# One attention-then-FFT-convolution kernel: pair 3 turned in f32, no key or query rounded by GpSimd, the last two output tiles in halves, all steps in a new order

## The chip, the cores and the metric

The kernel runs on one core of one Trainium2 chip. The metric is the device time of one execution in microseconds, median over the runs. The engines of the core work side by side, each through its own queue in order: TensorE (PE in the profile, its weight loads PEld), VectorE (DVE), ScalarE (ACT), GpSimd (POOL) and SyncE (SP), which here only issues DMAs.

## What is computed

The reference has two parts. Each of the 4 batches has 8 heads of 768 rows and 64 columns. The first part is attention over chosen blocks: the mean key of each block of 64 rows gives a gate score per query, the three best blocks and the query's own block are kept, and the causal softmax runs over those alone.

```python
k_rep = k.reshape(B, H, 12, 64, D).mean(axis=3)
gate_scores = einsum('bhsd,bhnd->bhsn', q, k_rep)      # causal blocks only
sel = top 3 blocks of a query, and its own block
scores = where(mask & causal, q @ k.T / 8, -1e9)
x = softmax(scores) @ v                                # (4, 768, 512)
proj = x @ w_proj                                      # x1, x2, x3, 512 columns each
x2_conv = irfft(rfft(x2, axis=1) * rfft(filter_fft, axis=0), n=768, axis=1)
out = (x1 * x2_conv * x3) @ w_out                      # float32
```

## The kernel before

**Work and tiles.** Heads go in pairs: 16 pairs, four to a batch; pair p holds heads 2*dc and 2*dc+1 of batch b, p = 4*b + dc. A pair's keys and queries come as one f32 tile each (`l`, two DMAs, one per head; line 565), its values by GpSimd's queue as f16 (`lv`, line 558). The scores of a pair are made in three groups (`s3p` to `s3p+2`, lines 802 to 816): keys against queries, then a second product that adds the mask. Each group fills two wide PSUM tiles (tags A and B, one per head); ScalarE takes the exponential of each (`e`, line 822), GpSimd zeroes what lies above the diagonal (`a`, line 828), TensorE multiplies by the values (`p`, line 838), VectorE divides (`nr`, `nm`). `xt`, or `xp` and `xq`, turns the result; `f` folds it (line 890). Then a batch goes through projection (`x`, `x1_`, `x3_`), a real transform written as matrix products (`z`, `t`, `mc`, `m`, `w`), its inverse (`i`, `ic`, `iy`, `iz`), the gate (`gg`, `y`), and the output product (`o`, lines 1034 to 1041), its eviction (`oc`) and store (`od`). Steps `fr`, `ff`, `fz`, `h`, `su`, `sv` transform the filter once.

**Two ways to prepare a pair.** For the pairs in `TURNED` (line 158: 0, 1 and 2) the f32 tiles are turned on TensorE as they are: `kt` multiplies the keys by an identity with two columns more, which give the block sums (line 599), `kh` and `kq` evict, `qt` and `qc` do the same for the queries (lines 589 and 652), `tq` casts a copy to f16, and the gate product `g` takes f32 operands (line 760). For all other pairs the rows are rounded to f16 first: `kn` and `qn` (lines 664, 666, 720, 722) round, `kl` and `qr` (lines 672, 728) keep what the rounding lost, `kw`/`kv` and `qw`/`qv` turn on TensorE and evict (in some pairs one DMA, `kx` or `qx`, does it), `kp`/`kq` sum the blocks, and `g` is 15 f16 products (line 765).

**What sets the order.** Nothing is planned at build time: `ORDER`, a list of 1,432 names, is walked at the end (lines 1081 to 1087). `name:V`, `:A` or `:G` says which engine does the step, `/a` to `/d` which PSUM tile it writes, `zeros/d:40` issues 40 products of zeros. Each engine gets its steps in that order and waits inside them; so a step that waits holds all that stand behind it on its engine. SP issues the loads and stores in list order too. Ten tiles hold loaded keys and queries, eight hold exponentials.

Of the kernel before, what the change touches and what calls it, by code (L numbers as in the profile page):

```python
# [45 lines left out]
kn9:A qr8:V s17 xc0.2:A nr9:V kq8:V nm9:V kr8:G xc0.1:A mt6/d qw7.1/c xt4 e17.0:A x0.3/b z0.0.2:V
lw2.3:G z0.0.1:V e17.1:A kl9:V x0.4/a lk10 qv7.1:A a17.0:G xc0.3:V s15 a16.1:G xc0.4:A z0.0.3:V g7/b
z0.0.0:V mm6:A qx8 z0.1.0:G e15.0:A t0.0.0/a mx7:V x0.5/d e15.1:A a15.0:G t0.1.0/c z0.1.2:V
x1_0.0.0/b xc0.5:A a17.1:G mc0.0.0:V a15.1:G mc0.1.0:A s19 z0.1.3:V lq10 x1c0.0.0:A a16.0:G m0.1.0:V
qn9:A lv6:G p15.1/c m0.0.0:V t0.0.1/b kw8/a m0.0.3:V mc0.0.1:A p15.0/d z0.1.1:V p16.1 kv8:A p17.1  # L50
m0.0.1:V p16.0 nr11:V x1_0.1.1/b m0.1.3:V e19.0:A w0.0.0:G nm11:V p17.0 kp9/a x1c0.1.1:V e19.1:A
# [1070 lines left out]
```

## Time and profile before

| | |
|---|---|
| median of 3 runs | 227.08 us (226.75 to 228.03) |
| the profiled execution | 228.22 us, span from first to last instruction 226.5 us |
| busy: PE, DVE, ACT, POOL | 213.2, 203.0, 175.8, 135.9 us |
| mean granted clock of TensorE | 0.97 of full speed |
| q, k: DMA issues | 64 of 192 KB, 5.3 to 5.4 us to landing (median) |

Busy time is read beside the span; a busy PE is not one at its peak, since ends of matmuls are modelled. The granted clock is 1.00 at 2.4 GHz and 0.50 at 1.2 GHz. "s4" and the like are the steps named above; the trace shows lines, and the first product of such a step is a line 808 instruction.

### The profile page before, as it was taken

What the parts mean: (1) busy time and instruction counts of PE and PEld (TensorE: products, weight loads), DVE (VectorE), ACT (ScalarE), POOL (GpSimd) and SP (SyncE); (2) the same over time, 40 slices, a digit from 0 to 9 for tenths busy, and PEclk for the clock granted to TensorE, in tenths of its full rate; (3) what the DMA queues carried; (4) which work ended last, traced back from release to release, by engine and by line L of the source; (5) the groups of instructions that cost most, each with busy time, mean ns of one, the idle gap of its engine ahead of it and who ended that gap; (6) DMA issues with size and microseconds to landing.
All of it is one profiled execution on the core that took longest, in us unless ns stands there. A gap on an engine that the chain in (4) does not pass through costs nothing.

```text
span 226.5 us, 7238 instructions
## 1 busy us (share of the span) xinstructions
PE 213.2 (94%) x2799; PEld 138.1 (61%) x2799; DVE 203.0 (90%) x656; ACT 175.8 (78%) x281; POOL 135.9 (60%) x260
## 2 busy tenths in 40 slices
...
GB/s 167 265 243 218 213 189 205 168 197 110 97 83 73 147 126 98 184 81 139 212 156 138 205 148 152 126 195 83 135 40 163 96 36 93 142 46 1 157 128 228
DMA packets 104194, 32.19 MB, mean 142 GB/s; under 512 B 97248, under 2 KB 100320, under 8 KB 104160
## 3 DMA queue, kind: packets, MB, share of 16 engines
...
q0 software_dynamic: 27392, 5.25, 30.1%
...
## 4 chain that ended last, share of the span: by engine, by line
PE 67%; DVE 22%; DMA 4%; issue 2%; ACT 2%; SPq 1%; DVEq 0%; ACTq 0%
PE x2p L906 9%; PE op L1039 9%; PE x1p L1006 8%; PE x3p L1018 7%; PE sps L808 7%; PE o L838 6%; PE sps L814 4%; DVE kl L672 2%; DMA nat<-in_k_dram 2%; DVE xnat L861 2%; DMA nat<-in_q_dram 2%; DVE m L774 2%; PE yeo L967 2%; DVE sd L982 1%; PE mt L789 1%
## 5 line engine op out<-in xcount | busy, mean ns | idle before, releaser
L822 ACT ACTIVATE ex<-sps 128x896 f16<-128x896 f32 x96 | 85.1, 923 | 15.2 <-PE sps L814 14.1
L828 POOL TENSOR_SCALAR_AFFINE_SELECT ex<-ex 128x256 f16<-128x256 f16 x96 | 45.8, 489 | 33.5 <-ACT ex L822 31.4
L838 PE MATMUL o<-V,ex 128*128 128x65 f16 x672 | 29.3, 194 | 0.5 <-POOL ex L828 0.4
L838 PEld LDWEIGHTS <-ex 128*128 128x128 f16 x672 | 25.6, 98 | 5.4 <-POOL ex L828 0.5
L808 PE MATMUL sps<-TQ,KH 64*128 64x256 f16 (+2 forms) x352 | 27.9, 272 | 0.2
L558 POOL DMA_DIRECT2D V<-in_v_dram x32 | 27.5, 860 | 0.2
L808 PEld LDWEIGHTS <-KH 64*128 64x128 f16 x352 | 13.2, 95 | 13.8 <-issue 9.7
L1025 DVE TENSOR_TENSOR gg<-x1sb,x3p 128x384 f16<-128x384 f16 x32 | 17.3, 545 | 1.9 <-PE x3p L1018 1.6
L192 ACT COPY osb<-op 128x512 f32<-128x512 f32 x21 | 12.4, 592 | 7.8 <-PE op L1039 5.6
L814 PE MATMUL sps<-MT,E 32*128 32x256 f16 (+2 forms) x480 | 17.5, 229 | 0.0
L861 DVE TENSOR_TENSOR xnat<-o,rc 128x384 f16<-128x384 f32 x32 | 17.2, 547 | 0.2
L192 ACT CAST x1sb<-x1p 128x384 f16<-128x384 f32 x27 | 13.0, 493 | 5.0 <-PE x1p L1006 4.9
L1006 PEld LDWEIGHTS <-wp 128*128 128x128 f16 x128 | 11.5, 97 | 8.0 <-issue 0.8
L1018 PEld LDWEIGHTS <-wp 128*128 128x128 f16 x128 | 11.9, 98 | 6.9 <-DVE lt L776 0.2
L814 PEld LDWEIGHTS <-E 32*128 32x128 f16 x480 | 10.5, 93 | 9.1 <-issue 8.8
L192 ACT CAST yes<-yeo 128x384 f16<-128x384 f32 x23 | 10.6, 483 | 6.1 <-PE yeo L967 5.7
L774 DVE MAX8 m<-g 128x8 f32<-128x12 f32 x160 | 13.8, 156 | 1.2 <-PE g L765 0.7
L672 DVE SCALAR_TENSOR_TENSOR kl<-nat,kn 128x768 f16<-128x768 f32 x13 | 13.8, 1060 | 0.3 <-ACT kn L664 0.2
L991 POOL TENSOR_TENSOR mid<-sd 128x256 f16<-128x256 f16 x5 | 3.7, 735 | 16.3 <-DVE sd L982 16.3
L782 POOL TENSOR_TENSOR MN<-lt,ownm 128x120 f16<-128x120 f16 x12 | 5.8, 481 | 12.2 <-DVE lt L776 11.6
L728 DVE SCALAR_TENSOR_TENSOR qn<-nat,qn 128x640 f16<-128x640 f32 x13 | 10.9, 847 | 0.5 <-POOL qn L722 0.4
L695 PE MATMUL qw<-id,qn 128*128 128x128 f16 x55 | 5.3, 238 | 2.7 <-DVE qn L722 1.6
...
## 6 DMA issues: line engine op xcount, KB each, us to landing
nat<-in_q_dram SPq DMA_DIRECT2D x32, 192.0 KB, 5.3
nat<-in_k_dram SPq DMA_DIRECT2D x32, 192.0 KB, 5.4
...
```

Source lines behind the costliest of these rows:

```text
L192: {"A": nc.scalar.copy, "V": nc.vector.tensor_copy, "G": nc.gpsimd.tensor_copy, "S": nc.sync.dma_start}[eng](dst, src)
L558: nc.gpsimd.dma_start(v16[:, :, h, 0:D], v[b, 2 * dc + h].rearrange("(c p) d -> p c d", p=P))
L808: nc.tensor.matmul(t[x][:, col:col + w], lhsT=kh[rows, P * kc:P * (kc + 1)], rhs=every_other(tq, rows, q0, w), start=(col, kc) == part[0][:2],
L814: nc.tensor.matmul(t[x % 2][:, col:col + w], lhsT=E4[rows, P * kc:P * (kc + 1)], rhs=mt16.rearrange("p c s -> p (c s)")[rows, m0:m0 + w], ...
L822: nc.scalar.activation(ex[:, 0:W], st["s", n][h][:, 0:W], AF.Exp, bias=0.0, scale=EXPS)
L828: nc.gpsimd.affine_select(out=tri, in_=tri, compare_op=ALU.is_ge, fill=0.0, base=0, pattern=[[0, 2], [1, P]], channel_multiplier=-1)
L838: nc.tensor.matmul(st["o", s][:, qc, :], lhsT=ex[:, col:col + P], rhs=v16[:, kc, h, 0:65], start=not begun, stop=False, skip_group_check=True)
L861: nc.vector.tensor_tensor(xn, o[:, :, 0:D], rc.to_broadcast([P, SC, D]), op=ALU.mult)
L906: nc.tensor.matmul(pa, lhsT=st["xf", b, eo, dc][:, i], rhs=wp[1][:, dc, :], start=(dc == 0), stop=(dc == DC - 1))
L1006: nc.tensor.matmul(x1p, lhsT=wp[0][:, d2, dsl], rhs=chunks(st["xT", b, d2]), start=(d2 == 0), stop=(d2 == DC - 1))
L1018: nc.tensor.matmul(x3p, lhsT=wp[2][:, d2, dsl], rhs=chunks(st["xT", b, d2]), start=(d2 == 0), stop=(d2 == DC - 1))
L1039: nc.tensor.matmul(po, lhsT=st["yT", b, cc, i % 2][:, P * (i // 2):P * (i // 2 + 1)], rhs=wo[:, cc, :], start=(cc == 0), stop=(cc == DC - 1))
```

## The change

One constant and the list. `TURNED` becomes `range(4)`: pair 3 is prepared like pairs 0 to 2. So `kn3 kl3 kw3 kv3 kp3 kq3 qn3 qr3 qw3 qv3` go, and `kt3 kh3 kq3 qt3 qc3 tq3` come, in two halves each; `g3` changes its form. `kn4`, `kn5`, `qn6` and `qn13`, which GpSimd rounded, go to VectorE, ScalarE, VectorE and ScalarE. Other steps change engine too: among them `fz0.2`, `fz1.0`, `fz1.2` and 14 of the `iz` go from VectorE to GpSimd, 9 `iz`, 9 `mn` and 6 `y` from GpSimd to VectorE, `er` from VectorE to ScalarE. Two bursts of zeros (5 and 8 products) go. The output tiles 4 and 5 of the last batch are made, evicted and stored as halves of 256 columns (`o3.5.1`, `o3.5.0`, `o3.4.1`, `o3.4.0`), two of the four stores issued by ScalarE. All steps stand in a new order; below are its beginning, up to the thirteenth score group, and its end.

```diff
@@ ORDER @@
-zt:V sgn:V tv:G lq0.0 fv:G lk0.1 mnz0:V selr:G tc:V lk0.0 zeros/d:40 sa0:V id32:G lq0.1 sb0:V lk1
-vone1:G twf:G sa1:V vone0:G tws:A sel:G sd0:V rq0.0:A id16:V lf0 sb1:V gcon:G se0:A mnz1:V qt0.0/a
-rk0.1:V twn:V kt0.1/b rk0.0:A cos0:V lq1 qc0.0:A kt0.0/c sd1:V kh0.1:A rq0.1:A eb:G kq0.1:V ip0.0/a
-ip1.0/d se1:A kq0.0:V kh0.0:V qt0.1/b ie1.0:A cos1:V kt1.1/c qc0.1:A kr0:G er:V tq0.1:A lk2 g0/b
-iw1:G tq0.0:A kh1.1:V flip:G ie0.0:A lf1 kq1.1:A ip0.1/c ownm:G ip1.1/a mx0:V kt1.0/d ie0.1:A fr0/c
-kh1.0:A lq2 ie1.1:V mn0:G kq1.0:A exptab:A lv0:G mt0/d qt1.0/a mm0:V qt1.1/b ff0.1:V s1 qc1.1:A
-ix0:V vone2:G qc1.0:A selh:G kr1:V ix1:V lk3 kt2.1/b e1.1:A g1/a kh2.1:V tq1.1:A ff0.0:V e1.0:A lq3
-fr1/d mx1:V tq1.0:A a1.0:G s0 kq2.1:V ff1.1:V mn1:G a1.1:G mt1/b ff1.0:V qt2.0/a e0.0:A lv1:G
-qt2.1/c fz0.2:V lf2 kt2.0/d e0.1:A mm1:V iw0:V fz1.2:V zeros/b:5 kq2.0:V qc2.1:V a0.0:G s2 a0.1:G
-qc2.0:V lk4 vone3:G kr2:V p0.0/c fz1.0:V e2.0:A p0.1/a p1.0 kn3:V g2/b e2.1:A kl3:V kh2.0:A a2.0:G
-s3 mx2:V qn3:A a2.1:G lq5 p1.1 e3.0:A p2.1 qr3:V p2.0 kp3/b kw3/d nr0:V e3.1:A kq3:V nr1:V qw3.1/b
-nm1:V qv3.1:A mn2:V s5 a3.1:G nm0:V tq2.0:G tq2.1:A kv3:V mt2/c fr2/b e5.0:A lq4 a3.0:G fz0.0:V
-kr3:G e5.1:A xp0/d ff2.1:V qw3.0/a a5.0:G s4 lk5 mm2:V lw1.2:G qv3.0:A fz1.3:V a5.1:G xq0:V p3.0/c
-kn4:G e4.1:A p3.1/a ff2.0:V g3/d f0.0:V e4.0:A lq6 a4.1:G mx3:V f0.1:G p4.1 qn5:A s7 fz0.1:V a4.0:G
-lk6 p5.1 kl4:V lv2:G e7.1:A p4.0 p5.0 kw4/d nr3:V e7.0:A zeros/b:8 qn4:V mn3:V fz0.3:V qw4.0/b kv4:A
-a7.1:G nr2:V s6 nm3:V kn5:G qv4.0:A nm2:V lk7 mt3/a h1.0/d qr4:V lv3:G e6.1:A kp4/c h0.0/b qr5:V
-su0.2:A lq7 fz1.1:V e6.0:A a6.1:G sv0.2:V su0.0:A kq4:V kl5:V qw4.1/c su0.1:A s8 qn6:G mm3:V qv4.1:A
-sv0.1:V xp1/a e8.0:A h1.1/c kr4:G xq1:V h0.1/d e8.1:A lq8 qr6:V qw5.0/a su1.1:A a8.0:G sv0.0:V s9
-a8.1:G qv5.0:V lw0.1:G kp5/b sv1.1:V e9.1:A a6.0:G p6.1/a p7.1 a7.0:G p8.1 kq5:V kn6:V lw1.3:G
-e9.0:A p6.0/b p7.0 nr5:V f1.0:G p8.0 nm5:V su1.0:A lk8 s10 nr4:V kl6:V lw1.0:G qw5.1/c e10.1:A
-a9.0:G sv1.0:V g4/a a9.1:G lk9 mx4:V lw1.1:G qv5.1:A h0.2/d a10.1:G e10.0:A kw5/c lv4:G kr5:V h1.2/a
-su2.1:A kv5:V s11 lq9 su2.0:A kn7:V kp6/c nm4:V mn4:G qn7:A a10.0:G kq6:V sv2.1:V mt4/b kr6:G g5/c
-e11.1:A mm4:V p9.1/a sv2.0:V p10.1 e11.0:A xp2/b a11.1:G qr7:V lw0.3:G kw6/d xq2:A s12 lw0.0:G mx5:V
-kv6:A lw0.2:G qw6.0/b a11.0:G e12.0:A kl7:V p9.0/d lw2.2:G p10.0 p11.1 p11.0 e12.1:A mn5:G nr7:V
...
-x3_3.2.1/a od2.3 iz3.2.0:V x1c3.3.0:A iz3.3.2:V iz3.2.1:V o2.5/d gg3.2.1:V iz3.2.2:V x3_3.3.0/b
-oc2.5:A y3.2.1:V y3.3.1:V x1_3.2.0/a y3.1.1:V od2.5 gg3.3.0:V x3_3.2.0/d x1c3.2.0:A y3.0.1:V
-y3.3.0:G o3.1/b gg3.2.0:V y3.2.0:V oc3.1:A o3.0/d od3.1 o3.3/b oc3.0:A od3.0 o3.2/d oc3.3:A od3.3
-o3.5/b oc3.2:A od3.2 o3.4/d oc3.5:A od3.5 oc3.4:A od3.4
+zt:V sgn:V tv:G lq0.0 fv:G lq0.1 tc:V id32:G sa0:V lk0.0 zeros/d:40 mnz0:V vone0:G gcon:G sa1:V
+lk0.1 sb0:V lq1 id16:V sd0:V sb1:V se0:A rq0.0:V sd1:V ip1.0/a rq0.1:A qt0.0/b lk1 twf:G cos0:V
+se1:A selh:G qt0.1/c ie1.0:V rk0.0:A selr:G qc0.0:V ip1.1/d ip0.0/a lf0 qc0.1:A cos1:V vone1:G tws:A
+kt0.0/b ie0.0:A rk0.1:G exptab:A lf1 sel:G kt0.1/a kh0.0:V kq0.0:V iw0:G lk2 ip0.1/c ie1.1:V qt1.0/b
+kq0.1:V ie0.1:V qt1.1/d kr0:G ix1:V g0/c flip:G qc1.1:A qc1.0:A kh0.1:A vone3:G vone2:G ownm:G
+kt1.0/b mx0:V kt1.1/a ix0:V fr0/d lq2 kq1.1:A mn0:V kq1.0:A iw1:A tq0.1:V kr1:G mnz1:V kh1.0:A eb:G
+mt0/c ff0.0:V fr1/b mm0:A kh1.1:A ff0.1:V lk3 lv0:G tq0.0:A g1/a ff1.1:V er:A twn:V s1 lk4 fz1.2:G
+mx1:V kt2.1/d e1.0:A tq1.0:V mn1:G kt2.0/a ff1.0:V lq3 e1.1:A fz1.0:G qt2.0/c kh2.1:V qt2.1/b
+kq2.1:V kq2.0:V qc2.0:A kh2.0:V s0 a1.1:G qc2.1:A kr2:V tq2.0:G mt1/b a1.0:G g2/a e0.0:A fz0.2:G
+e0.1:A lf2 kt3.1/c mx2:V mm1:A s2 a0.1:G kq3.1:A a0.0:G tq1.1:V lq4 p0.1/a tq2.1:G e2.1:A kh3.1:V
+p0.0/b p1.1 kt3.0/d mn2:V kn4:V e2.0:A a2.1:G p1.0 mt2/c kl4:V p2.1 kh3.0:A s5 kq3.0:A a2.0:G mm2:V
+lk5 nr1:V lv1:G p2.0 nm1:V e5.0:A qt3.0/c nr0:V qt3.1/d qc3.0:V fr2/a e5.1:A fz0.0:V lq5 nm0:V
+qc3.1:A a5.1:G s3 tq3.0:A ff2.0:V tq3.1:G qn4:A ff2.1:V kr3:G xp0/d a5.0:G kp4/b lk6 e3.0:A xq0:V
+lv2:G g3/c fz1.3:V e3.1:A fz1.1:V fz0.3:V h1.0/d qr4:V su0.2:A s4 lw1.3:G f0.0:V kq4:A a3.1:G mx3:V
+kw4/b a3.0:G e4.1:A p3.1/a kr4:G lq6 e4.0:A p3.0/c f0.1:V a4.1:G fz0.1:V kn5:A s7 a4.0:G qn5:V lv4:G
+lk7 kl5:V p4.1 e7.1:A p4.0 p5.1 p5.0 qr5:V e7.0:A mn3:G nr2:V nr3:V nm2:V su0.0:A s6 a7.0:G nm3:V
+lv3:G kn6:A kv4:V mt3/c xp1/a e6.1:A mm3:V h0.0/b lq7 xq1:V kp5/c e6.0:A sv0.0:V a6.1:G h1.1/a
+lw0.3:G kq5:A sv0.2:V su1.0:A s8 a7.1:G lw0.2:G kl6:V su0.1:A h0.1/c e8.1:A a6.0:G lk8 sv0.1:V
+qw4.0/b f1.1:G e8.0:A sv1.0:V qw4.1/d lw2.0:G qv4.1:V qv4.0:A s9 lw1.0:G f1.0:V qn6:V su1.1:A p6.1/b
+a8.1:G g4/d e9.1:A a8.0:G sv1.1:V kw5/c kr5:G p7.1 e9.0:A mx4:V lq8 p8.1 p6.0/a a9.1:G p7.0 p8.0
+kv5:A s10 nr5:V kn7:V mn4:G nr4:V nm5:V kp6/c a9.0:G e10.0:A mt4/d nm4:V lw1.2:G qw5.1/b qr6:V
+qw5.0/a kq6:A qv5.1:A h0.2/c a10.0:G mm4:V e10.1:A xp2/b kl7:V lw1.1:G h1.2/d su2.1:A kr6:G s11
+xq2:V lk9 qv5.0:A qn7:V kw6/b f2.1:G e11.1:A sv2.1:V g5/a mx5:V su2.0:A a10.1:G a11.1:G e11.0:A
+p9.1/d lv5:G lk10 p10.1 sv2.0:V p11.1 kv6:A p9.0/a s12 nr7:V kn8:V nm7:V a11.0:G qw6.1/b e12.1:A
...
+oc2.3:A y3.1.0:V o2.5/b iz3.2.1:V od2.3 x1c3.2.1:A iz3.3.1:V x1c3.3.1:A iz3.2.2:G x3_3.2.1/c
+y3.0.1:V x1_3.3.0/a iz3.3.2:G gg3.2.1:V oc2.5:A x3_3.3.0/d y3.0.0:V y3.2.1:G x1c3.3.0:V od2.5
+x3_3.3.1/b gg3.3.0:V y3.1.1:G x1_3.2.0/a gg3.3.1:V x3_3.2.0/d y3.3.0:V x1c3.2.0:A y3.3.1:V o3.1/b
+gg3.2.0:V y3.2.0:V oc3.1:V o3.0/d od3.1 o3.2/b oc3.0:A od3.0 o3.3/d oc3.2:A od3.2 o3.5.1/b oc3.3:A
+o3.5.0/a od3.3 o3.4.1/d oc3.5.1:V o3.4.0/c oc3.5.0:V od3.5.1:A od3.5.0 oc3.4.1:A oc3.4.0:V od3.4.1
+od3.4.0:A
@@ -155,7 +157,7 @@
-    TURNED = range(3)
+    TURNED = range(4)
```

## Rows read from the trace of the kernel before

**Rows 1.** The page, part 1: busy time of each engine, share, instructions.

```profile
PE 213.2 (94%) x2799; PEld 138.1 (61%) x2799; DVE 203.0 (90%) x656; ACT 175.8 (78%) x281; POOL 135.9 (60%) x260
```

**Rows 2.** Four stretches: length, busy per engine, clock, DMA share, GB/s.

```profile
0.00:27.86 27.86, 26.41 (x320) 21.66 (x321) 23.07 (x98) 21.06 (x37) 17.77 (x64) 1.00 1.17 221
27.86:57.07 29.21, 23.52 (x383) 16.49 (x382) 27.15 (x68) 21.80 (x30) 24.85 (x39) 0.77 1.16 172
57.07:222.78 165.71, 163.29 (x2101) 99.99 (x2099) 152.76 (x492) 132.35 (x215) 93.27 (x159) 1.00 0.80 123
222.78:226.50 3.72, 0.00 (x0) 0.00 (x0) 0.00 (x0) 0.59 (x1) 0.00 (x0) 1.00 0.50 186
```

**Rows 3.** The same view, three stretches of 6 us inside the second.

```profile
30.00:36.00 6.00, 4.54 (x76) 3.65 (x75) 5.90 (x16) 3.94 (x5) 6.00 (x8) 0.71 1.16 198
36.00:42.00 6.00, 3.90 (x45) 2.37 (x46) 5.31 (x14) 3.50 (x5) 2.69 (x4) 0.50 1.75 201
42.00:48.00 6.00, 6.00 (x78) 3.61 (x77) 4.87 (x10) 4.32 (x7) 5.16 (x9) 0.65 0.84 171
```

**Rows 4.** Instructions of DVE in order: start us, duration us, line, out<-in.

```profile
28.17 1.54 DVE L441 TENSOR_TENSOR xz__503<-xz__503,x__733 128x512 f16<-128x512 f16 x1
...
30.10 0.67 DVE L478 TENSOR_TENSOR x__793<-osb,rev 128x512 f16<-128x512 f32 x1
30.70 1.87 DVE L890 TENSOR_TENSOR xf__812<-xT__771 128x384 f16<-128x384 f16 x1
...
34.04 2.07 DVE L672 SCALAR_TENSOR_TENSOR kl<-nat,kn 128x768 f16<-128x768 f32 x1
...
37.08 0.41 DVE L441 TENSOR_TENSOR xz__487<-xz__487,x__793 128x512 f16<-128x512 f16 x1
...
41.73 0.95 DVE L672 SCALAR_TENSOR_TENSOR kl<-nat,kn 128x768 f16<-128x768 f32 x1
```

**Rows 5.** Instructions of POOL in the same time, the same columns.

```profile
28.58 2.17 POOL L666 TENSOR_SCALAR kn<-nat 128x768 f16<-128x768 f32 x1
...
31.07 0.91 POOL L890 TENSOR_TENSOR xf__833<-xT__771 128x384 f16<-128x384 f16 x1
...
34.46 2.16 POOL L666 TENSOR_SCALAR kn<-nat 128x768 f16<-128x768 f32 x1
```

**Rows 6.** Groups by line and form: busy us, mean ns, idle before, releaser.

```profile
L435 POOL TENSOR_TENSOR xz__1857<-x__1808,x__1833 128x512 f16<-128x512 f16 x1 | 1.2, 1217 | 0.4 <-ACT x__1833 L192 0.4
```

**Rows 7.** DMA issues of the page, then what queue q1 moved in 26 and 28 us.

```profile
nat<-in_q_dram SPq DMA_DIRECT2D x32, 192.0 KB, 5.3
...
q1 hardware_dynamic: 14040, 5.39, 93.0%
...
q1 hardware_dynamic: 15443, 5.75, 92.4%
```

**Rows 8.** Groups by line: ScalarE's exponentials and its query roundings.

```profile
L822 ACT ACTIVATE ex<-sps 128x896 f16<-128x896 f32 x96 | 85.1, 923 | 15.2 <-PE sps L814 14.1 <-POOL kr L748 0.6 <-POOL ex L828 0.3
...
L720 ACT ACTIVATE qn<-nat 128x768 f16<-128x768 f32 x8 | 6.9, 857 | 0.0
```

**Rows 9.** TensorE's weight loads and products of single steps, in order of time.

```profile
12.20 0.64 PEld L589 LDWEIGHTS qt<-ids,nat 128*128 128x128 f32 x6
...
13.80 0.74 PEld L599 LDWEIGHTS kt<-ids,nat 128*128 128x128 f32 x6
...
21.03 1.19 PEld L760 LDWEIGHTS g<-bd,q 128*128 128x128 f32 x10
...
24.14 0.34 PEld L684 LDWEIGHTS <-kn 128*128 128x128 f16 x6
...
30.23 0.47 PEld L765 LDWEIGHTS <-TQ 128*128 128x128 f16 x15 [0.97 <-issue]
...
34.40 1.06 PE L1079 MATMUL z<-zt 128*128 128x128 f16 x8
```

**Rows 10.** The chain of waits, its last piece: start, duration, what.

```profile
222.84 0.59 ACT osb L192
```

More of the change, by code (lines that the diff above doesn't have):

```diff
@@ L46 @@
[L46 to L51, printed above, removed]
@@ new lines @@
+e14.0:A x0.0/b a14.1:G xc0.1:A p14.1 a14.0:G xc0.0:V s16 kn9:A lv7:G z0.0.2:V p14.0 z0.0.0:V e16.1:A
+kp8/b nr8:V x0.2/d kq8:V nr9:V nm8:V e16.0:A kr8:G qw7.0/b qw7.1/a kl9:V xc0.2:A lw2.1:G s17 qv7.1:A
+lv6:G qv7.0:V x0.5/d e17.1:A z0.0.3:V nm9:V t0.0.0/b e17.0:A mt6/a qn9:V xt4 x0.4/c a16.0:G xc0.5:V
+mm6:A a16.1:G s15 qr9:V xc0.4:A mc0.0.0:A a17.0:G kw8/c z0.0.1:V qx8 e15.1:A g7/a a17.1:G z0.1.1:V
+x0.3/b lw2.3:G e15.0:A m0.0.3:V lw2.2:G mx7:V t0.1.0/d a15.1:G xc0.3:A lq10 s19 a15.0:G mc0.1.0:A
@@ new lines @@
+z0.1.0:V lo.0:G kn10:A p15.1/a m0.1.0:V p15.0/d kv8:V p16.1 e19.1:A x1_0.1.1/b m0.0.0:V mn7:V p17.1
+z0.1.2:V x1c0.1.1:A p16.0 nr11:V p17.0 z0.1.3:V e19.0:A x1_0.0.0/c nm11:V t0.0.1/b nr10:V m0.1.3:V
+x1c0.0.0:A t0.2.1/a a19.0:G nm10:V mc0.0.1:A s20 f4.0:V mc0.2.1:A xt5 m0.0.2:V mt7/b m0.0.1:V
+t0.2.0/d e20.0:A w0.0.1:V kp9/a w0.0.0:V lk11 x1_0.0.1/c mc0.2.0:A m0.2.2:V m0.2.1:V mm7:A
+x3_0.1.1/d m0.2.3:V kq9:A x1c0.0.1:A m0.2.0:V t0.1.1/a e20.1:A kr9:G lq11 gg0.1.1:V x1_0.1.0/c
+kl10:V mc0.1.1:A lv8:G g8/d x1c0.1.0:A s18 qn10:A w0.2.0:V w0.2.1:V m0.1.1:V kw9/c qx9 e18.1:A
@@ new lines @@
+a20.1:G mx8:V x3_0.1.0/a w0.1.0:G x3_0.0.0/b kv9:A gg0.1.0:V lq12 x1_0.3.0/d a18.1:G e18.0:A
+gg0.0.0:V a19.1:G x1_0.2.0/a m0.1.2:V lv9:G x1c0.3.0:A mn8:V f5.0:V kn11:A s21 w0.1.1:V f5.1:V
+x1c0.2.0:A qr10:V i0.0.0/d e21.1:A i0.1.1/b i0.1.0/a ic0.0.0:V p18.1/c lk13 ic0.1.0:A p19.1
+ic0.1.1:V a21.1:G p20.1 e21.0:A i0.3.0/d a20.0:G nr13:V i0.0.1/b iy0.1:V x1_0.3.1/a ic0.0.1:A
+a21.0:G ic0.3.0:A s22 iz0.1.0:V a18.0:G nm13:V x1c0.3.1:A iy0.0:V p18.0/c e22.1:A mt8/a iz0.1.1:V
+i0.3.1/d p19.0 iz0.0.0:V iz0.1.2:G p20.0 ic0.3.1:V e22.0:A x3_0.0.1/b f4.1:V iz0.0.1:G nr12:V
```

147 lines of the change are left out of this document (68 added, 79 removed).

## The prediction

> **What bounds the kernel now.** I read the busy shares first, then stretches cut at three score groups, then the instructions of the worst stretch, then the loads and the end. The busy shares [rows 1] show TensorE at 94% and VectorE at 90%: both look like the bound, and an average can't say where. The stretches [rows 2] are cut where the sixth score group to run starts (s4, at 27.86), where the thirteenth starts (s12, at 57.07), and where the last product ends (222.78). Here the reader sees three different kernels. From 57.07 on TensorE is busy for 163.29 of 165.71 us at the full clock (2.4 GHz): only 2.4 us can be had there without taking products away. Between 27.86 and 57.07 TensorE is busy for 23.52 of 29.21 us, at a mean clock of 0.77, while VectorE is busy for 27.15. So there VectorE is the bound, and a slow TensorE stands beside it. The 3.72 us behind the last product are eviction and store.
>
> Inside the second stretch [rows 3], VectorE has 5.90 of 6 us from 30 on, GpSimd 6.00, TensorE falls to 4.54 and 3.90, and its clock goes to the lower level (0.50, 1.2 GHz); it comes back by 48, after a stretch in which TensorE was busy throughout. By the means (0.71, 0.50, 0.65, full elsewhere) the half clock lasted about 3.5 + 6 + 4.2 = 13.7 us.
>
> Why VectorE is full is in its instructions beside GpSimd's [rows 4, 5]. An f16 addition that takes 0.41 at 37.08 takes 1.54 at 28.17, while GpSimd's rounding of keys runs (28.58, 2.17). The rounding error of pair 4's keys takes 2.07 at 34.04 beside the next rounding (34.46, 2.16), against 0.95 at 41.73. The fold at 30.70 takes 1.87 beside a fold on GpSimd (0.91 at 31.07); it is shorter work than the 0.41 addition. That is 1.1 + 1.1 + 1.4 = 3.6 us in which VectorE did nothing useful. At 30.10 the addition that reads PSUM takes 0.67 in the same time, and shows no such loss.
>
> **The change, part by part.** *No rounding on GpSimd.* The 1.1 + 1.1 go. The 1.4 goes as well, because both folds of that pair go to VectorE; that adds 0.4. The four roundings themselves become two on VectorE and two on ScalarE, 0.86 each on ScalarE [rows 8]. What is late next: GpSimd isn't empty, since three filter additions come to it. By the one row of this kind, 1.22 each [rows 6], 3.7 us stand between the triangles of pairs 0 and 1.
>
> The Trainium skill (GPSIMD Engine Reference, Key points) says that GpSimd shares its SBUF interfaces with VectorE and collides with VectorE instructions that have two SBUF inputs or use both ports. The trace agrees as far as it goes: 0.41 became 1.54 with two SBUF inputs, and the one with an input from PSUM kept 0.67 [rows 4]. By that rule the three filter additions and the 14 `iz` moved to GpSimd collide again: it speaks against the change, and it is the second rival below.
>
> *Pair 3 in f32.* TensorE gains two key halves of 0.74, queries of 0.64, a gate of 1.19 instead of 0.47, and loses 17 f16 transposes (6 take 0.34, so 1.0) and 12 tiny sums (0.3, an estimate by the 15 small gate products at 0.47) [rows 9]: 1.48 + 0.64 + 0.72 - 1.3 = +1.5 us. The zeros that go took 1.06 at half clock, and 5 more at full clock about 0.3 [rows 9]. All of it lies ahead of s12, where TensorE has room, so by itself it is worth nothing in time; bounds +1.5 (if TensorE becomes the bound there) and -1.4 (the zeros, if they were on the path). VectorE loses five steps, among them a rounding error of 0.95 [rows 4], and gets two evictions.
>
> *The new order, first stretch.* List position alone doesn't give a time; the loads do. Query loads are two issues of 192 KB [rows 7]. In the new list SP issues up to pair 4's queries: eight tensors of pairs 0 to 3, the filter (1.57 MB), k4 and q4, in all 5.51 MB. Before, q5 stood ahead of q4. Queue q1 had moved 5.39 MB at 26 and 5.75 at 28 [rows 7], so q4 is there at about 26.7. Now `qn4` on ScalarE stands directly ahead of the exponentials of s3, and s4 needs the PSUM tiles which those read: 26.7 + 0.3 (landing, estimated) + 0.86 + 2 x 0.92 [rows 8] = 29.7 for s4, against 27.86: +1.8. Queued behind the waiting rounding on ScalarE are those exponentials, and behind them GpSimd's triangles and TensorE. If q4 is earlier than that, the step costs nothing; if other queues take a tenth of the rate, it is 2.7 us more.
>
> *The new order, s4 to s12.* In the same stretch of steps VectorE loses 18 and gets 10. The difference, at 0.41 to 0.95 a step [rows 4], is about -3.6, and with the 3.6 of collisions its 27.15 become 20. On ScalarE seven steps leave and eight come, all between a few tenths and 0.86 [rows 8]: 21.80 become about 21. The longer of the two, with the 3 us that each waits for the others (ScalarE's exponentials waited 14.1 us for scores in the whole run [rows 8]), gives 24 instead of 29.2. Lower end 21, no wait at all; upper end 29, if what is saved is waited for elsewhere. So s12 comes at 29.7 + 24 = 53.7 instead of 57.07: -3.4.
>
> *TensorE's clock.* Its work from s4 to s12 is about 16.5 us at full clock: 23.52 less half of the 13.7, since it was partly idle then, with -0.5 for the steps moved. In 24 us that is a share of 69%, before it was 58%. Whether the clock falls again no row can tell. If it is half for h us and TensorE is then never idle, s4 to s12 takes h + (16.5 - h/2)/0.69 = 24 + 0.275 h. I put +0.7, a fall of 2.5 us; ends 0 and +6.6 (24 us of it).
>
> *After s12.* TensorE has the same products; a few moved ahead of s12: -0.5. Its idle 2.4 can grow or shrink with the new order; I leave it, with -2 and +3 as ends. The moved `iz` and `y` are hidden by TensorE as long as it has work queued; if that cover goes, it is within these ends.
>
> *Halves at the end.* Before, the last eviction of 512 columns took 0.59 [rows 10], then came issue, 256 KB of transfer and the finish, 3.7 us in all [rows 2]. A half needs perhaps two thirds of that eviction (-0.2) and half of the transfer, which at the 186 GB/s of that stretch [rows 2] is at most 0.7; I take -0.2 of it, because the fixed part isn't shortened. Together -0.4, ends -0.9 and +0.3 (two more issues).
>
> **Sum.** -3.4 - 0.5 - 0.4 + 0.7 = -3.6 us, on a span of 226.5: 222.9. The profiled execution took 228.22 with that span, 1.1 us over the median of the runs shown, so I take the difference to the median: 227.08 - 3.6 = **223.5 us**.
>
> **Rivals.** *The clock falls as long as before.* For it: TensorE still waits for others, and the 13 products of zeros that filled its waits are gone. Against: pair 3's f32 products come where it was idle. With h = 13.7 the stretch takes 27.8: 3.8 more than 24, 0.7 of which is in the sum, so 226.6.
>
> *Collisions come back.* For it: three additions on GpSimd ahead of s4, 14 `iz` later, and the fold at 30.70 lost 1.4 to one addition of 0.91 [rows 4, 5]. Against: VectorE's neighbours of the filter additions mostly read PSUM (`ff`, `mx`, `kh`), and 24 steps leave GpSimd for VectorE (9 `iz`, 9 `mn`, 6 `y`). Half of 3 x 1.4 ahead of s12 is 2.1: 225.6.
>
> *The last stretch gives it back.* The order behind s12 has 3 us more of TensorE idle, while the front gains as forecast: 226.5 or more.
>
> *Slower.* ScalarE's wait for q4, with s4 behind it, leaves TensorE idle at 27 to 30; the clock falls there, earlier than before, and stays low until s12. Then TensorE's 16.5 us take 33, s12 comes at 62.7, 5.6 after its old time, and with -0.9 from the rest the kernel takes 231.8. It decides from h = 16: 29.7 + 24 + 0.275 x 16 = 58.1, which the later parts just offset. For it: in the old kernel the clock fell behind waits of this kind [rows 3]. Against: a TensorE at half clock is then always busy, and in the trace such a stretch ended the low clock.
>
> **Chances.** Forecast (221 to 225.5) 0.53; clock 0.14; collisions 0.11 (on top of a forecast else right); last stretch 0.09; slower 0.13. What can be told from no change here is about 0.5%, 1.1 us: faster is below 225.9, slower above 228.2. Faster: 0.53 + 0.07 of the collisions + 0.06 of the clock case + 0.02 = 0.68. Slower: 0.13 + 0.03 from the ends of the last stretch = 0.16. Same: 0.16. The range for 8 of 10 goes from 219.5 (a middle stretch of 21 and a good last one) to 228.0.
>
> **What would show it.** In the changed kernel's profile no GpSimd instruction of 2.1 us stands, and VectorE has no 1.5 us additions between 28 and 50. s4 starts near 29.7, later than before, with ScalarE idle or its `qn4` waiting on the q load; s12 starts near 53.7. The half clock lasts under 5 us. From s12 to the last product it is 165 us, and 3.3 from there to the end. The prediction is wrong in its middle if s12 isn't before 56, in its clock if the half clock lasts over 10 us, and in its last part if TensorE idles for over 5 us after s12.

## The result, and the profile after

The changed kernel takes **223.88 us** (median of 4 runs, 223.43 to 224.42) against 227.47 for the kernel before (4 runs): a ratio of 0.9842, 95% interval 0.9809 to 0.9875. 223.5 was forecast, in a range of 219.5 to 228.0. The total is right, in part by luck: s12 came 1.75 us earlier than the sum had it, the end lost 1.3 us against its term, and the two nearly cancelled.

The page's part 1 of the changed kernel, which answers to [rows 1], and below it the same four stretches as in [rows 2], cut where s4 and s12 start and where the last product ends. (Lines of the changed kernel are two higher than before: the exponentials are L824.)

```profile
PE 209.3 (94%) x2778; PEld 136.5 (61%) x2778; DVE 198.6 (89%) x652; ACT 173.0 (78%) x280; POOL 137.3 (62%) x265
```

```profile
0.00:29.94 29.94, 28.31 (x328) 23.37 (x329) 24.29 (x101) 21.24 (x39) 22.41 (x68) 1.00 1.13 223
29.94:52.62 22.68, 18.27 (x358) 13.11 (x358) 22.45 (x69) 20.75 (x32) 21.58 (x41) 1.00 1.47 214
52.62:218.00 165.38, 162.70 (x2096) 99.97 (x2093) 151.46 (x484) 130.63 (x210) 93.33 (x158) 1.00 0.81 121
218.00:222.60 4.60, 0.00 (x0) 0.00 (x0) 0.42 (x1) 0.37 (x1) 0.00 (x0) 1.00 0.47 159
```

| us | before | forecast | after |
|---|---|---|---|
| s4 starts | 27.86 | 29.7 | 29.94 |
| s4 to s12 | 29.21 | 24, and 0.7 for the clock | 22.68 |
| s12 to the last product's end | 165.71 | 165.2 | 165.38 |
| from there to the end | 3.72 | 3.3 | 4.60 |
| span | 226.5 | 222.9 | 222.6 |

The gain is in the second stretch: VectorE is busy for 22.45 us there instead of 27.15, with one instruction more, and waits for 0.2 us. The clock column reads 1.00 in all four. The next three rows answer to [rows 3].

```profile
30.00:36.00 6.00, 3.83 (x85) 2.90 (x85) 5.96 (x19) 5.00 (x9) 5.65 (x12) 1.00 1.55 216
36.00:42.00 6.00, 4.71 (x66) 2.73 (x66) 6.00 (x12) 5.86 (x10) 6.00 (x10) 1.00 1.86 199
42.00:48.00 6.00, 5.87 (x134) 4.70 (x134) 5.97 (x23) 5.21 (x8) 5.41 (x13) 1.00 1.26 246
```

From 30 to 36 TensorE is *less* busy than before (3.83 us against 4.54, part of which ran at half clock), and its clock stays at the upper level all the same.

VectorE's instructions after (start, duration, line) answer to [rows 4]. The filter additions (L443) are at 0.41 now. Two large collisions are left. The fold at 30.60 takes 1.18, beside two of GpSimd's triangles (L830); the pair's other fold takes 0.35 at 32.80. And the rounding error in the last row takes 1.83 (0.95 undisturbed), beside a fold of 1.64 us on GpSimd that VectorE does in 0.34 (`f1.0`, at 43.05).

```profile
28.86 0.41 DVE L443 TENSOR_TENSOR xz__420<-xz__420,x__711 128x512 f16<-128x512 f16 x1
...
30.60 1.18 DVE L892 TENSOR_TENSOR xf__783<-xT__741 128x384 f16<-128x384 f16 x1
...
32.80 0.35 DVE L892 TENSOR_TENSOR xf__837<-xT__741 128x384 f16<-128x384 f16 x1
...
34.09 1.16 DVE L674 SCALAR_TENSOR_TENSOR kl<-nat,kn 128x768 f16<-128x768 f32 x1
...
39.57 1.83 DVE L674 SCALAR_TENSOR_TENSOR kl<-nat,kn 128x768 f16<-128x768 f32 x1
```

```profile
30.77 0.80 POOL L830 TENSOR_SCALAR_AFFINE_SELECT ex<-ex 128x256 f16<-128x256 f16 x2
...
40.53 1.64 POOL L892 TENSOR_TENSOR xf__1030<-xT__963 128x384 f16<-128x384 f16 x1
```

That s4 comes 2.08 us later is decided ahead of the first score group, s1, which starts at 13.01 before and at 15.24 after. The rows are the stretch up to s1 and the one from s1 to s4, first before, then after:

```profile
0.00:13.01 13.01, 11.76 (x102) 10.45 (x102) 9.60 (x47) 8.80 (x19) 8.91 (x41) 1.00 0.93 225
13.01:27.86 14.85, 14.65 (x219) 11.21 (x219) 13.47 (x52) 12.26 (x19) 8.86 (x24) 1.00 1.37 217
```

```profile
0.00:15.24 15.24, 13.71 (x115) 11.76 (x117) 11.88 (x48) 9.56 (x20) 10.30 (x48) 1.00 0.94 234
15.24:29.94 14.70, 14.60 (x214) 11.61 (x214) 12.40 (x54) 11.68 (x19) 12.11 (x21) 1.00 1.33 211
```

The end is where the change lost. Below are the changed kernel's evictions after the last product (by ScalarE and VectorE) and the chain of waits there. They wait 2.29 and 1.70 us for a store. The ring of output buffers has four places, so o3.4 goes where o3.0 was, and the store of o3.0 took 4.07 us to land.

```profile
219.20 0.37 ACT L194 COPY osb<-op 128x256 f32<-128x256 f32 x1 [2.29 <-DMA out_dram<-osb]
219.29 0.42 DVE L194 COPY osb<-op 128x256 f32<-128x256 f32 x1 [1.70 <-DMA out_dram<-osb]
```

```profile
214.42 0.59 ACT osb L194
215.01 0.02 issue
215.03 4.07 DMA out_dram<-osb
...
219.29 0.42 DVE osb L194
```

### The profile page after: what moved, and what is told of

It reads as the page before. It is cut to its first block, busy times and chain, and to the rows that moved or that the text cites. A ratio compares the mean times of both kernels' runs of the same rounds, so it can differ in the third digit from the quotient of the medians.

```text
span 222.6 us, 7204 instructions
## 1 busy us (share of the span) xinstructions
PE 209.3 (94%) x2778; PEld 136.5 (61%) x2778; DVE 198.6 (89%) x652; ACT 173.0 (78%) x280; POOL 137.3 (62%) x265
## 4 chain that ended last, share of the span: by engine, by line
PE 55%; POOL 19%; DVE 10%; issue 5%; DMA 4%; SPq 3%; ACT 2%; DVEq 0%; POOLq 0%; ACTq 0%
PE x3p L1020 8%; PE x1p L1008 7%; PE op L1041 7%; POOL ex L830 7%; PE x2p L908 6%; PE o L840 6%; PE sps L810 5%; POOL V L560 5%; PE sps L816 3%; POOL wp L508 3%; DMA tn__263<-in_moe_filter_fft_dram 2%; PE yeo L969 2%; DMA out_dram<-osb 2%; PE kt L601 1%; SPq L567 1%
## 5 line engine op out<-in xcount | busy, mean ns | idle before, releaser
L824 ACT ACTIVATE ex<-sps 128x896 f16<-128x896 f32 x96 | 85.0, 922 | 12.3 <-PE sps L816 11.2
L830 POOL TENSOR_SCALAR_AFFINE_SELECT ex<-ex 128x256 f16<-128x256 f16 x96 | 45.5, 486 | 36.4 <-ACT ex L824 35.1
L840 PE MATMUL o<-V,ex 128*128 128x65 f16 x672 | 30.5, 193 | 3.4 <-POOL ex L830 1.2
L560 POOL DMA_DIRECT2D V<-in_v_dram x32 | 28.4, 889 | 0.3
L810 PE MATMUL sps<-TQ,KH 64*128 64x256 f16 (+2 forms) x352 | 27.0, 267 | 1.0 <-ACT ex L824 1.0
L194 ACT COPY osb<-op 128x512 f32<-128x512 f32 (+1 forms) x21 | 11.9, 579 | 13.3 <-PE op L1041 10.9
L998 POOL TENSOR_TENSOR sd<-sd,mid 128x256 f16<-128x256 f16 x10 | 7.1, 716 | 19.9 <-DVE sd L995 19.9
L194 ACT CAST x1sb<-x1p 128x384 f16<-128x384 f32 x28 | 13.6, 488 | 5.5 <-PE x1p L1008 3.9
L674 DVE SCALAR_TENSOR_TENSOR kl<-nat,kn 128x768 f16<-128x768 f32 x12 | 13.1, 1095 | 0.0
L194 ACT CAST yes<-yeo 128x384 f16<-128x384 f32 x19 | 8.7, 485 | 1.6 <-PE yeo L969 1.0
L743 POOL TENSOR_TENSOR bd<-krs,ids 128x24 f32<-128x24 f32 x13 | 3.8, 289 | 6.6 <-ACT krs L194 4.4
L666 ACT ACTIVATE kn<-nat 128x768 f16<-128x768 f32 x9 | 7.7, 860 | 0.0
```

Source lines behind the costliest of these rows:

```text
L194: {"A": nc.scalar.copy, "V": nc.vector.tensor_copy, "G": nc.gpsimd.tensor_copy, "S": nc.sync.dma_start}[eng](dst, src)
L560: nc.gpsimd.dma_start(v16[:, :, h, 0:D], v[b, 2 * dc + h].rearrange("(c p) d -> p c d", p=P))
L810: nc.tensor.matmul(t[x][:, col:col + w], lhsT=kh[rows, P * kc:P * (kc + 1)], rhs=every_other(tq, rows, q0, w), start=(col, kc) == part[0][:2],
L824: nc.scalar.activation(ex[:, 0:W], st["s", n][h][:, 0:W], AF.Exp, bias=0.0, scale=EXPS)
L830: nc.gpsimd.affine_select(out=tri, in_=tri, compare_op=ALU.is_ge, fill=0.0, base=0, pattern=[[0, 2], [1, P]], channel_multiplier=-1)
L840: nc.tensor.matmul(st["o", s][:, qc, :], lhsT=ex[:, col:col + P], rhs=v16[:, kc, h, 0:65], start=not begun, stop=False, skip_group_check=True)
```

## The experiments

The kernels were timed in three groups, each together with the kernel before, and ratios are to that, with 95% intervals. It took 227.47 us with the four roundings (off and back), the two whole tiles and the buffers of their own; 227.92 with pair 3 alone, the zeros, the filter additions and pair 4; 227.79 with the other four. A ratio is known to about 0.3%, so two kernels of different groups are told apart from about 0.5%, 1.1 us. The diffs show only the steps that change, and `...` stands for what lies between.

**The four roundings alone, in the old order.**

```diff
-kn4:G  kn5:G  qn6:G  qn13:G
+kn4:V  kn5:A  qn6:V  qn13:A
```

> The kernel before with only kn4, kn5, qn6 and qn13 taken off GpSimd (to VectorE, ScalarE, VectorE, ScalarE), order and everything else as it was. Theory (collisions): VectorE gets back 2.2 us, pays about 1.2 for its two roundings, TensorE's wait of 1.6 us for qw4.0 shrinks, the half clock lasts shorter than 13.7 us: 1.5 to 2.5 us faster (225 to 226). Rival: without the new order the time is waited for elsewhere: within 0.5 us of the kernel before.

225.23 us, 0.990 (0.987 to 0.993): 2.2 us faster, as the collision theory said. VectorE's busy time from s4 to s12 falls from 27.15 to 25.62 us although it rounds twice itself. The three instructions of [rows 4] that stood beside GpSimd's work give back 0.81, 0.77 and 0.91 us:

```profile
28.81 0.73 DVE L441 TENSOR_TENSOR xz__503<-xz__503,x__733 128x512 f16<-128x512 f16 x1
...
30.99 1.10 DVE L890 TENSOR_TENSOR xf__812<-xT__771 128x384 f16<-128x384 f16 x1
...
33.50 1.16 DVE L672 SCALAR_TENSOR_TENSOR kl<-nat,kn 128x768 f16<-128x768 f32 x1
```

Two things keep this from being a clean price of the collisions. The fold still has GpSimd's fold and triangles beside it, as before, so its 0.77 can't be put down to a rounding. And the half clock fell as well, from 10.4 to 3.6 us in the middle of the runs; by the run with zeros (below) that is worth 0.5 us of the 2.2, 1.4 at most.

**The same roundings back on GpSimd, in the new order.**

```diff
-kn4:V  kn5:A  qn6:V  qn13:A
+kn4:G  kn5:G  qn6:G  qn13:G
```

> The changed kernel with kn4, kn5, qn6 and qn13 back on GpSimd, in the places that they have in the new list. Theory (collisions): each rounding takes 2.16 us on GpSimd, which has 1.1 us to spare between s4 and s12, and VectorE's neighbours lose 1.1 us each: s12 comes 3 to 5 us later, the kernel takes 227 to 229. Rival: the new order is what counts, VectorE loses the two roundings it had and waits elsewhere: within 0.7 us of 223.9.

229.17 us, 1.0068 (1.0039 to 1.0097): 5.3 us above the changed kernel, and slower than the kernel before. The size fits the theory, the mechanism only in part. In its stretch from s4 to s12 VectorE is busy for 22.66 us, 0.2 more than after, though one of its roundings (0.6 to 0.8) is gone, so collisions cost it about 1 us there; GpSimd is busy for 24.75 of 25.26. The waits of TensorE and VectorE between 20 and 57 us (total, times, longest) show what it cost:

```profile
31.01:56.27 25.26, 19.59 (x359) 14.07 (x359) 22.66 (x68) 20.03 (x31) 24.75 (x43) 0.93 1.30 196
```

```profile
PE o L840 <- POOL ex L830: 3.5, 3, 1.3
...
DVE kl L674 <- POOL kn L668: 2.0, 2, 1.3
```

The rounding (2.13 and 2.52 us here) stands in GpSimd's row ahead of triangles, and TensorE waits 3.5 us for these (0.4 after); VectorE waits 2.0 for the rounding itself. Of the span, 1.1 us are lost ahead of s4, 2.6 from s4 to s12 and 1.2 behind it. So a slow instruction on GpSimd had two prices: collisions where VectorE stood beside it, and the place in GpSimd's row where the order has filled that row.

**Pair 3 alone, in the old order.**

```diff
-    TURNED = range(3)
+    TURNED = range(4)
-kn3:V kl3:V qn3:A qr3:V kp3/b kw3/d kq3:V qw3.1/b qv3.1:A kv3:V qw3.0/a qv3.0:A
+kt3.0/b kt3.1/d kh3.0:V kq3.0:V qt3.1/b qc3.1:A kh3.1:V kq3.1:V qt3.0/a tq3.1:G qc3.0:A tq3.0:G
```

> The kernel before with pair 3 turned in f32 in the places of its old steps, the four roundings left on GpSimd and the order otherwise as it was. Forecast's term: nothing in time by itself, with TensorE 1.5 us more to do where it has room. Theory now: VectorE is full between s4 and s12 but pair 3's steps stand mostly ahead of s4, so within 0.7 us of the kernel before (227.5). Rival: pair 3 is the part that makes the changed kernel fast, 1.5 us or more faster; the f32 products also keep TensorE's clock up (mean clock 0.99 or more instead of 0.97 to 0.98).

227.75 us, 0.9995 (0.9971 to 1.0019): nothing, as forecast. In its profile two effects cancel: s4 starts 1.0 us later, and s4 to s12 takes 27.65 us instead of 29.21, with VectorE busy for 25.51 instead of 27.15. So pair 3's steps do weigh on VectorE behind s4, other than expected. The half clock also went down (5.9 us in the middle of the runs), and no time came with it.

**Both parts in the old order.**

> The kernel before with both parts: the four roundings off GpSimd (alone 1.0% faster) and pair 3 turned in f32 in its old places (alone no change); the order otherwise as it was. If the parts add up, it takes what the roundings alone gave, 225.2 to 225.7, and the rest of the change's gain, some 2 us, is the new order with the steps that change engines. Rival: each frees what the other waits for; together they give most of the whole change, 224 or less.

224.95 us, 0.9874 (0.9842 to 0.9906): they add up, 1.3% against 1.0% for the roundings alone, which is hardly told apart. So about 2.8 of the change's 3.6 us need no new order, as far as intervals of 0.7 us to either side allow.

**Zeros in place of a wait, in the kernel before.**

```diff
-zeros/b:8
+zeros/b:20
```

> The kernel before with the second burst of zeros 20 instead of 8 products long, nothing else: it fills the 1.63 us in which TensorE waited for the queries of pair 4 at half clock. Theory (the clock costs time by itself): the half clock ends earlier than at 46 us; over the runs of the kernel before the span grows by 0.23 us with each us of half clock, so 3 to 10 us less of it make the kernel 0.7 to 2.3 us faster. Rival: the half clock only stands beside VectorE's work, which sets the pace; the mean clock may rise, the time stays within 0.5 us, or grows by up to 0.5 where the zeros stand in front of the queries.

227.16 us, 0.9982 (0.9954 to 1.0009). The half clock of a run is 2 x (1 - mean clock) x span. In the 44 runs of the kernel before in the first two groups it lasted from 3.6 to 13.6 us, 10.4 in the middle; the profile that the forecast rests on was at the long end. With the zeros the middle is 4.9, and the time changes by -0.4 us (between -1.1 and +0.2). That is 0.07 us for each us of half clock, 0.2 at most. The zeros themselves held nothing up: in the profiles the queries of pair 4 are turned at 37.07, and at 37.09 without them.

From run to run the picture isn't uniform. Within the 12 runs with zeros a higher clock bought nothing: the three at a mean of 0.998 took 227.32 to 228.06, the five at 0.985 from 226.81 to 229.13. But a line through the 44 runs of the kernel before has 0.15 us per us, and with the roundings off GpSimd the two runs with at most 0.4 us of half clock took 224.25 and 224.28, the nine with 3.6 from 224.95 to 226.38. Such runs may differ in more than the clock, so they give no price.

In the profile with zeros the clock came back at 35 and fell again at 42:

```profile
30.00:36.00 6.00, 5.42 (x88) 4.56 (x87) 5.90 (x16) 3.93 (x5) 6.00 (x8) 0.72 1.07 169
36.00:42.00 6.00, 3.04 (x55) 2.01 (x54) 6.00 (x14) 4.38 (x7) 3.24 (x5) 0.99 1.66 201
42.00:48.00 6.00, 6.00 (x104) 4.03 (x98) 5.28 (x10) 4.34 (x6) 5.83 (x10) 0.72 1.06 215
```

In the first two rows VectorE is full (5.90 and 6.00 of 6 us): a slow TensorE there does its work inside waits that it would have anyway. One wait shows it, TensorE's for `krs` (block sums that VectorE evicts), first in the kernel before, then with zeros. At full clock TensorE gets there earlier and waits longer:

```profile
41.87 0.71 PE L695 MATMUL qw<-id,qn 128*128 128x128 f16 x5 [1.01 <-DVE krs L192]
```

```profile
41.30 0.45 PE L695 MATMUL qw<-id,qn 128*128 128x128 f16 x5 [1.92 <-DVE krs L192]
```

In the third row it is the other way round: TensorE is busy for 6.00 of 6 us, much of it at half clock, and VectorE for 5.28. There the half clock can cost time, in both kernels.

**The last two tiles whole.**

```diff
-o3.5.1/b oc3.3:A o3.5.0/a od3.3 o3.4.1/d oc3.5.1:V o3.4.0/c oc3.5.0:V od3.5.1:A od3.5.0 oc3.4.1:A oc3.4.0:V od3.4.1 od3.4.0:A
+o3.5/b oc3.3:A od3.3 o3.4/d oc3.5:A od3.5 oc3.4:A od3.4
```

> The changed kernel with the last two output tiles whole, evicted by ScalarE and stored by SyncE, as in the kernel before. If the halves cost the 0.9 us, it is 0.9 us faster (223.0). If it is the buffer that the last eviction waits for, the whole tile waits for the same store, until about 219.1, and the kernel is as slow or 0.3 us slower (223.9 to 224.2). If the halves are worth the 0.4 us forecast and something else made the end longer, it is 0.4 us slower.

**223.09 us** (222.45 to 223.63), 0.9806 (0.977 to 0.9843): the best of all kernels run, 0.8 us under the change. The two were timed in different groups and their intervals overlap, so the times alone hardly show it. The profile does: the end is 3.7 us, as before the change, with no wait for a store.

**Buffers of their own for the halves.**

```diff
-st["osb", b, i] = buf("osb", SC * b + i, 4, (P, Dm), FP32)
+st["osb", b, i] = buf(f"tn{i - 4}_", 0, 1, (P, Dm), FP32)
```

> The changed kernel, with buffers of their own for the halves of the last two output tiles (two that the filter used long before), nothing else. Theory: the 0.9 us by which the end grew is the wait of the last two evictions for the store of o3.0 and o3.1, whose buffers they reuse; without it they follow the last product at 218.0 at once, and the kernel is about 1.2 us faster (222.7 against 223.9). Rival A: the stores are held by the transfer itself (1.28 MB from 214.9 to 219.4), the last two then only move up to its end: 0.6 us faster. Rival B: the end is the price of four stores instead of two, no change.

223.56 us, 0.9821 (0.9782 to 0.9859): 0.3 us under the change, not told apart from it. The evictions no longer wait for a store, yet the end is 4.3 us, because the stores still land late (the halves in 2.6 to 3.2 us, where whole tiles take 2.0). The wait for the buffer was mostly a symptom.

**All half stores from SyncE.**

```diff
-od3.5.1:A ... od3.4.0:A
+od3.5.1 ... od3.4.0
```

> The changed kernel with buffers of their own for the last halves (223.56, end 4.3 us, stores 2.6 to 3.3 us to landing), all four half stores issued by SyncE. If it is the second queue that makes the stores beside it slow, they land in 2.0 to 2.3 us, as whole ones do, and it is 0.5 us faster (223.0). If it is the pieces of half the size, landing stays near 3 us and the time within 0.3 us of 223.56 or, with one more issue in SyncE's row, 0.2 us above.

223.61 us, 0.981 (0.9783 to 0.9837): the same. The second queue isn't it: with one queue three of the four whole stores ahead of the halves took 4.1, 3.7 and 3.5 us. The halves landed in 2.1 to 2.6, but they were issued later.

**One tile in halves, stored whole; four steps back on VectorE.**

```diff
-fz0.2:G fz1.0:G fz1.2:G f1.1:G
+fz0.2:V fz1.0:V fz1.2:V f1.1:V
-o3.5.1/b ... od3.4.0:A
+o3.5/b oc3.3:A od3.3 o3.4.1/d oc3.5:A od3.5 o3.4.0/c oc3.4.1:A oc3.4.0:V od3.4
```

> The changed kernel with fz0.2, fz1.0, fz1.2 and f1.1 on VectorE, the tile o3.5 whole, and o3.4 computed and evicted in halves by two engines but stored in one piece. If the slow stores of 128 KB made the end longer and the split of the product and the eviction is harmless, the end is 3.5 us long or a little under (4.6 after, 3.7 with whole tiles), and the kernel takes 222.5 to 223.0. If splitting the product itself is at fault, the end stays over 4 us and the time near 223.5.

224.27 us, 0.9835 (0.9807 to 0.9863): the hope fell. All stores are of 256 KB and one queue issues them, and still the end is 4.7 us and the store of o3.0 takes 3.96. So it is not the size of the stores either. What the slow ends share is in the DMA view: a load of instructions (a transfer on the queue that the page calls `instruction`) beside the last stores. First the changed kernel from 213 us to its end (GB/s in 40 slices of 0.24 us, then queues with packets and MB), then the one with whole tiles (slices of 0.205 us):

```profile
GB/s 0 0 0 0 0 0 0 0 9 350 384 350 376 358 333 17 341 358 350 86 324 393 337 333 201 329 205 26 26 21 43 311 333 350 81 0 0 0 0 0
...
q1 hardware_dynamic: 864, 1.31, 37.8%
q10 hardware_dynamic: 288, 0.26, 8.3%
q8 instruction: 1, 0.02, 0.8%
```

```profile
GB/s 0 0 0 0 0 0 0 0 270 400 350 350 400 370 370 50 80 410 370 370 60 360 370 400 140 350 370 400 160 220 360 400 290 10 0 0 0 0 0 0
...
q1 hardware_dynamic: 864, 1.57, 51.1%
```

In the changed kernel the rate falls to 21 to 26 GB/s for three slices, from about 219.5. That is one sixteenth of the 393 reached with all 16 engines, which suggests that a single engine is still at its share while the others are done. The load took 1.2 us of one engine (0.8% of 16 engines' 9.6 us) and began at 216.85. The profiles of all 14 kernels of this case have such loads. In the seven whose last tile is split, one begins 1.0 to 2.0 us ahead of the last product's end, among the last stores, and the ends are 4.3 to 5.0 us long. In the seven with whole tiles the ends are 3.7 to 3.8 us. There the load begins 4.3 to 7.3 us ahead of the last product's end, and of the last six stores it touches at most the first, or it doesn't come before the end: with whole tiles and the changed kernel's list otherwise as it is, it comes at 222.95, behind the span.

The late landing doesn't need the split. From 200 us on the 14 profiles hold 126 stores with no load of instructions beside them, which landed in 1.7 to 2.9 us (half of them within 2.04). The 43 with such a load took 2.0 to 4.1 (half of them over 3.4); the nine under 2.5 had it only at their start or end. The kernel with 20 zeros has whole tiles, and its store issued at 213.20, beside a load at 214.60, took 3.8 us; the next one, issued at 215.41, took 2.2. First the store at 213.20, then the window from 214.5 to 215.7:

```profile
out_dram<-osb SPq DMA_DIRECT2D x1, 256.0 KB, 3.8
```

```profile
q8 instruction: 1, 0.02, 4.9%
...
out_dram<-osb SPq DMA_DIRECT2D x1, 256.0 KB, 2.2
```

**qn4 behind the exponentials.**

```diff
-qn4:A ... e3.0:A ... e3.1:A
+e3.0:A ... e3.1:A qn4:A
```

> The changed kernel with qn4 behind the exponentials of s3 instead of ahead of them on ScalarE. The recorded prediction put s4 at 29.7 because those exponentials wait behind qn4 for q4's load: then s4 now comes 0.9 us earlier or more (29.0) and the kernel gains some of it. Rival: s4 stands behind TensorE's own row, which the trace after shows busy from 18 to 30 us: s4 stays at 29.9, the time within 0.5 us of 223.88.

224.07 us, 0.9833 (0.9805 to 0.9862): no change. s4 starts at 29.50, but s0 already started 0.46 earlier than after (18.10 against 18.56), and from s3 to s4 it is 2.96 us here and 2.95 after. In the changed kernel's own profile `qn4` (L722) runs without a wait, ahead of the exponentials, so q4 was there in time:

```profile
27.28 0.52 ACT L194 CAST TQ<-q 128x384 f16<-128x384 f32 x1
27.68 0.86 ACT L722 ACTIVATE qn<-nat 128x768 f16<-128x768 f32 x1
28.42 1.73 ACT L824 ACTIVATE ex<-sps 128x896 f16<-128x896 f32 x2
```

**GpSimd's filter additions and a fold on VectorE.**

```diff
-fz0.2:G fz1.0:G fz1.2:G f1.1:G
+fz0.2:V fz1.0:V fz1.2:V f1.1:V
```

> The changed kernel with fz0.2, fz1.0, fz1.2 and f1.1 on VectorE instead of GpSimd. If GpSimd's work beside VectorE still costs it (a kl of 1.83 us beside f1.1's 1.64 us, an xf of 1.18), VectorE gets 1.5 us back for 1.6 us of new work and GpSimd, full between s4 and s12, has 5 us less: 0.5 to 1 us faster. Rival: VectorE is full as well (22.45 of 22.68 us), the four steps go on top: 0.5 to 1.5 us slower.

223.52 us, 0.9826 (0.9792 to 0.986): not told apart from the change. The 1.83 us rounding error is at 0.95 again, and VectorE's busy time from s4 to s12 falls to 21.71; the stretch itself takes 22.43 instead of 22.68. The three filter additions say nothing about collisions. After, they ran on GpSimd at 15.39, 17.41 and 19.78 for 1.15 us each, and no instruction of VectorE with two SBUF inputs stood beside them; the one that reads PSUM, at 17.10, took its usual 0.68. TensorE is also busy there for 14.60 of the 14.70 us from s1 to s4, so little could show.

**Pair 4 turned as well (with whole tiles).**

```diff
-    TURNED = range(4)
+    TURNED = range(5)
-kn4:V kl4:V qn4:A qr4:V kp4/b kq4:A kw4/b kv4:V qw4.0/b qw4.1/d qv4.1:V qv4.0:A
+kt4.0/b kh4.0:A kq4.0:V kt4.1/b kh4.1:V kq4.1:V qt4.0/b qt4.1/d qc4.1:V qc4.0:A tq4.1:V tq4.0:V
```

> The changed kernel with the last output tiles whole and pair 4 turned in f32 too, in the places of its old steps. VectorE loses a rounding of keys, two rounding errors and an eviction (some 3 us between s5 and s9) and gets five short steps (some 2 us); TensorE gets 1.5 us where it idles for 4.4 of 22.7 us. If the same exchange is what helped with pair 3: 0.5 to 1 us faster than whole tiles alone (222.1 to 222.6). Rival: f32 evictions come at points where TensorE's next product waits, and q4's tile is held longer: 0.5 to 1.5 us slower (223.6 to 224.6).

223.93 us, 0.9844 (0.9811 to 0.9876): 0.8 above whole tiles alone, as the rival said, though the two intervals overlap; faster it isn't. From s4 to s12 VectorE is busy for 21.54 us instead of 22.45, and the stretch takes 23.26 instead of 22.69. TensorE has 19.47 us to do there instead of 18.50, and its waiting shrinks by only 0.4 us, from 4.19 to 3.79. So it doesn't take up the new work where it idled, as it would have to: it now waits 0.6 us for VectorE's `krs` ahead of one f32 turn, and 0.3 for another eviction ahead of the next.

## Why the prediction came out, step by step

**No rounding on GpSimd: right, and the largest part.** 2.2 us of the change's 3.6 come with these four steps alone. The forecast charged 3.6 us of VectorE's time to the three collisions; 2.5 came back, and 0.8 of this is the fold. In the changed kernel it still takes 1.18, with both folds on VectorE, so the working was wrong to count its 1.4 as gone. The Trainium skill (GPSIMD Engine Reference, Key points) has VectorE instructions with two SBUF inputs collide with GpSimd, and the three rows, all with two SBUF inputs, agree with it (0.41 became 1.54). The second rival expected the filter additions to collide by that rule; nothing with two SBUF inputs stood beside them. A full row on GpSimd, which was the larger price in the new order, stood in no term.

**Pair 3: right in time, wrong in place.** Nothing by itself, but not because TensorE had room ahead of s12. Alone it made s4 1.0 us later and the stretch behind it 1.6 us shorter.

**s4 at 29.7: right number, wrong reason.** I said that `qn4` waits for q4's load and holds the exponentials of s3. It waits for nothing, and moving it changes nothing. The 2 us are there at s1 already (15.24 against 13.01), where q4 plays no part: the new list puts the second filter transform (`fr1`) and the gate product `g1` ahead of s1, and TensorE is busy there for 13.71 us instead of 11.76. From s1 to s4 it has no room in either kernel (14.65 of 14.85, 14.60 of 14.70). The working had put all of TensorE's added time where it "has room"; ahead of s4 it had none. That the load's sum gave the same 29.7 is luck.

**s4 to s12 in 24 us: better, 22.68.** I took ScalarE's 21 us as the longer, with VectorE at 20, and added 3 us of waiting. ScalarE was right at 20.75, but VectorE needed 22.45, of which some 1.9 are the collisions left (0.83 at the fold, 0.21 and 0.88 at the rounding errors), and it waited 0.2. For VectorE, which set the pace, the 24 amount to 20 of work and 4 of waiting: 2.5 us too little and 3.8 too much. With the end of no wait at all (21) the direction was covered.

**The clock, +0.7: none of it came.** There was no half clock in the profile. Its price of 0.275 us per us isn't borne out by the zeros either, which put it at 0.07, 0.2 at most. The working assumed that at half clock "TensorE is then never idle"; before, it was busy for 10.68 of the 13.65 us of half clock, and for 3.90 of 6 from 36 to 42 [rows 3]. The same assumption took half of the 13.7 us off its work and made that 16.5 us; at full clock it is 18.27. The first rival (226.6) priced the clock in the same way and would cost about 1 us, 2.7 at most, by the zeros' price.

**After s12, -0.5: about right,** -0.33 in this profile, and about -1 in the profiles of the variants that keep its order behind s12 (164.4 to 164.8 us).

**Halves, -0.4: wrong sign.** The end grew by 0.9, and with whole tiles it is 3.7 us again. I priced the eviction and the bytes of a store, and put two more issues at +0.3. That a load of instructions can lie beside the last stores and make them land late stood in no term.

**The sum.** s12 came 4.45 us earlier instead of 3.4, the last stretch gave 0.3, the end took 0.9 back: -3.9 in the span, -3.6 in the medians. Of the parts, the roundings and pair 3 give about 2.8 us, the rest of the new order some 1.5 (0.9874 to 0.9806), the halves take 0.8 back, each known to about 1 us.

**What stays open.** Why the clock stays up after. Before, TensorE was busy for 3.27 of the 4.5 us ahead of the fall at 32.5; after, for 2.13 of 4 from 32 to 36, and the clock stayed. With `qn4` moved it was busy for 2.46 of 4.1 ahead of 38.1, and there the clock fell for 3.4 us. The busy time doesn't tell these apart, and one moved step was enough to bring the fall back in a profile. What a us of half clock costs is open too: the zeros give a small price, and the runs with the roundings off go with a larger one. And the load of instructions goes with the slow stores in all 14 profiles, but it was never moved by itself: a kernel with whole tiles and just so many more instructions that the load falls among the last stores was not tried.
